# An attention and state-space kernel: other TensorE work is placed into planned waits as soon as it can go, and its allowance counts each round's products

## The chip, the core and the metric

The kernel runs on one core of a Trainium2 chip. The metric is device time in microseconds (us) from the launch to the end of the program. Three runs of the kernel before took 1277.9, 1279.32 and 1282.04 us; the median is 1279.32 us. The engines are called PE (TensorE), DVE (VectorE), ACT (ScalarE), POOL (GpSimd) and SP (SyncE, which issues most transfers). Each takes its instructions strictly in the order in which the program lists them.

## What is computed

Two unrelated results are joined side by side: `outa`, a long convolution whose filter comes from a state-space model, and `outb`, attention with 32 heads that share one set of keys and values.

```python
# a: D = 576 channels, L = 2048 positions, N = 128 states
K = einsum("dn,dnl,dn->dl", Cc, exp(dt * A * l), dB).real   # complex powers: exp, sin, cos
y = irfft(rfft(u, 2L) * rfft(K, 2L))[:L] + u * Dskip
# b: S = 2048 positions, 32 heads of 18, one k and one v for all heads
q = x @ wq;  k = x @ wk;  v = x @ wv
o = softmax(q k^T * 18**-0.5) v
out = concat([y, o.reshape(S, 576) @ wo], -1)
```

## The kernel before

**The attention in rounds.** The attention is cut into 1024 tiles: 4 chunks of 512 queries, 16 pairs of heads in each, and 16 blocks of 128 keys. For each tile PE computes two 128x512 scores into a PSUM tile `s` (`scores`, L384, two matmuls), ACT takes their exponentials into `P` (`exponentials`, L392), and for every two tiles PE multiplies `P` by the values into `ops` (`product`, L664, four matmuls). There are three `s` buffers (NS) and six `P` buffers (NP). The loop in `main` therefore goes by rounds of three tiles: three scores, one or two products (a product takes two tiles, so the rounds alternate), and the exponentials. The scores of a round wait for the exponentials of the round before to free their `s` buffers.

**Other work.** Everything else has to find a place beside this. On PE these are pieces of 0.1 to 0.75 us by the program's own costs: the query projections (`q`, L157), the output projections (`op`, L157), the filter tables of the convolution (`kg`, L976), and the transforms of its signal and filter (`hu`, `lu`, `hk`, `lk`, `iy`, L157). They share one PSUM bank, `ps_f`: a piece that begins a new result has to wait until DVE has read the one before out of it. DVE carries most of the convolution as long rows of elementwise instructions. The convolution goes by 12 blocks of 48 channels. For each block ACT has to leave the exponentials once and compute a cosine and a sine (`r` at L905, `f` at L906), with a table load ahead of them and another one behind (L905, L392).

**The order of the work.** PE, DVE and ACT run an order that the program writes out itself while it is built. Generators yield after every piece, and `Stream` wraps one of them: `side` (query projections and output projections), `prep` (scaling of finished heads), and two for the convolution (`front` for the filter of the next block, `back` for the current one). What a generator yields is a kind, a time from which the next piece is ready, and whether it holds the bank. Kind "p" is a piece for PE, "v" for DVE, "w" waits for a later round, and "b" is the cosine and sine, which `Conv.go` lets go as soon as at least 8 pieces of projections are in hand (`beside`), or after 16 key blocks. A `Clock` estimates the time of PE, DVE and ACT (`K.t`, `K.v`, `K.a`); `K.fill` is when the shared bank is free, by this estimate. DVE's estimate is 0.085 us for an instruction and 1.04 ns for each element of a row (`Clock.dve`, `Vector`).

**Where other work is put.** `fill(then)` is called ahead of every product and ahead of each round's scores; `then` is when that next step can go. It offers the streams their turn until none can go. Pieces for PE need credit: an allowance that each round raises (the rest of TOTAL spread over the rest of the loop, within bounds) and each piece lowers, or time that is left before `then`. A stream whose next piece is not ready at `K.t` is passed over, and is not looked at again until the next call, which may be behind the next scores. RATE and PACE say how much DVE work of the convolution may be, and should be, done by each step.

**The end.** When the loop is over, the last products are issued, then whatever is left of the output projections, and then `finish`, which scales the last heads (`rc_last`, L521 and L511 on DVE) and adds the last parts of `outb`.

## Time and profile before

| what | value |
|---|---|
| median of three runs | 1279.32 us |
| the profiled execution | 1282.59 us, span from first to last instruction 1280.8 us |
| PE busy | 1174.6 us, 92% of the span |
| ACT busy | 1045.9 us, 82% |
| DVE busy | 991.2 us, 77% |
| POOL busy | 226.6 us, 18% |
| mean granted TensorE clock | 0.972 of full speed |

A row of the timeline gives the start, the time that the instructions take together, the engine, the line, what is written and read, and in square brackets how long the engine had been idle and what ended that. Two program matmuls of this kind count as four in it (x4): the trace counts each float32 matmul twice, except those of the scores. Starts are more reliable than ends on PE, since matmuls overlap and their ends are modelled. A row of the windows gives for each engine the busy time and the count in a stretch, then the granted clock and the transfers.

The first scores start 33.6 us after the span's start, the last ones at 1261.3 us.

### The profile page before, as it was taken

The page shows a single profiled execution, that of the slowest core. Times are in us where ns is not written, and L with a number is a line of the kernel's source. Part 1 is how long each engine was busy: PE and PEld are TensorE (multiplying, and loading weights), DVE is VectorE, ACT ScalarE, POOL GpSimd, SP SyncE. Part 2 cuts the span into 40 slices and gives each one's busy share as a digit, 9 for nine tenths or more (in the row PEclk, how much of TensorE's full clock was granted, in tenths as well). Part 3 has the DMA queues.
Part 4 walks back from the last instruction along what each step waited for, and adds up shares of the span by engine and source line. Part 5 has one row for each costly group of instructions (what it writes and reads, how often), then busy time and mean ns, then how long its engine had stood idle before and what let it go on. Part 6 is the DMA issues. An engine that isn't in the chain of part 4 may idle for free.

```text
span 1280.8 us, 32948 instructions
## 1 busy us (share of the span) xinstructions
PE 1174.6 (92%) x13762; PEld 481.4 (38%) x13762; DVE 991.2 (77%) x1612; ACT 1045.9 (82%) x1101; POOL 226.6 (18%) x450
## 2 busy tenths in 40 slices
PE   5799799899999899999899899899899999899997
PEld 1234234334334344344334344334344334333433
DVE  4565985896797887897798887897795797798673
ACT  2488987898998888988788888788887978987884
POOL 3262002214110030230051030041050120020000
PEclk9799899899999899999899899899999999999999
DMA  7522013012021011212023012022012212012111
GB/s 216 173 50 60 14 37 104 22 57 73 24 67 58 19 48 64 64 39 98 18 73 99 10 38 74 10 77 80 17 38 96 78 36 68 21 26 74 51 39 40
DMA packets 56922, 75.35 MB, mean 59 GB/s; under 512 B 19536, under 2 KB 30160, under 8 KB 56256
## 3 DMA queue, kind: packets, MB, share of 16 engines
q1 hardware_dynamic: 35784, 58.22, 13.8%
q0 software_dynamic: 20288, 14.39, 5.1%
q8 instruction: 110, 1.80, 0.6%
q10 hardware_dynamic: 696, 0.58, 0.1%
q14 instruction: 44, 0.36, 0.1%
HBM read 35.28 MB, written 22.54 MB: 45 GB/s over the span
## 4 chain that ended last, share of the span: by engine, by line
PE 64%; ACT 15%; issue 10%; DVE 5%; DMA 3%; SPq 1%; POOL 1%; ACTq 0%; DVEq 0%; POOLq 0%
PE ops L664 27%; PE s L384 19%; ACT P L392 12%; PE op L157 5%; PE q L157 5%; PE iy L157 2%; PE kg L976 2%; DVE tab L95 2%; DMA xr<-xT 2%; SPq L265 1%; ACT L392 1%; ACT f L906 1%; PE hu L157 1%; PE lu L157 1%; PE hk L157 1%
## 5 line engine op out<-in xcount | busy, mean ns | idle before, releaser
L392 ACT ACTIVATE P<-s 128x1024 f32<-128x1024 f32 x1024 | 967.2, 1032 | 200.5 <-PE s L384 175.1
L664 PE MATMUL ops<-P,v_sb 128*32 128x512 f32 x4096 | 544.4, 606 | 3.7 <-DVE o L99 2.9
L384 PE MATMUL s<-aug,kaug 55*128 55x512 f32 x2048 | 378.6, 450 | 79.0 <-ACT P L392 75.3
L384 PEld LDWEIGHTS s<-aug,kaug 55*128 55x128 f32 x2048 | 174.4, 187 | 379.6 <-ACT P L392 335.1
L348 POOL DMA_DIRECT2D aug<-qh x252 | 126.4, 510 | 677.6 <-DVE qh L99 428.1
L664 PEld LDWEIGHTS ops<-P,v_sb 128*32 128x32 f32 x4096 | 109.8, 110 | 130.3 <-issue 92.0
L157 PE MATMUL q<-x,wq_sb 128*32 128x256 f32 (+2 forms) x1480 | 112.2, 417 | 0.0
L157 PE MATMUL op<-wo_sb,oT 126*32 126x288 f32 (+1 forms) x1152 | 88.7, 421 | 1.0 <-DVE part L99 0.3
L374 POOL DMA_DIRECT2D aug<-sh x61 | 33.0, 548 | 231.4 <-DVE sh L103 231.3
L157 PEld LDWEIGHTS q<-x,wq_sb 128*32 128x32 f32 (+1 forms) x1480 | 48.8, 115 | 65.2 <-issue 41.6
L348 POOL DMA_DIRECT2D aug<-ql x128 | 65.0, 514 | 5.1 <-issue 5.1
L99 DVE COPY ksb<-kg 128x192 f32<-128x192 f32 x48 | 17.5, 364 | 56.1 <-PE kg L976 56.1
L95 DVE TENSOR_TENSOR tab<-tab,tt 128x576 f32<-128x576 f32 (+1 forms) x72 | 59.1, 821 | 1.7
L95 DVE TENSOR_TENSOR tab<-tab 128x576 f32<-128x576 f32 (+1 forms) x72 | 59.0, 819 | 1.1
L95 DVE TENSOR_TENSOR tab<-sum,r 128x576 f32<-128x576 f32 (+1 forms) x72 | 58.8, 816 | 0.0
L95 DVE TENSOR_TENSOR tt<-f,sum 128x576 f32<-128x576 f32 (+1 forms) x72 | 58.7, 815 | 0.0
L95 DVE TENSOR_TENSOR tab<-r,dif 128x576 f32<-128x576 f32 (+1 forms) x72 | 58.6, 814 | 0.0
L157 PEld LDWEIGHTS op<-wo_sb,oT 126*32 126x32 f32 (+1 forms) x1152 | 34.1, 112 | 59.9 <-issue 28.4
L95 DVE TENSOR_TENSOR sck<-lk,sck 128x384 f32<-128x384 f32 x48 | 24.5, 552 | 31.7 <-PE lk L157 31.7
L95 DVE TENSOR_TENSOR acc<-acc,pt 128x1728 f32<-128x1728 f32 (+2 forms) x36 | 48.6, 1350 | 0.2
L95 DVE TENSOR_TENSOR pt<-us,ks 128x1728 f32<-128x1728 f32 (+2 forms) x36 | 48.6, 1350 | 0.1
L976 PEld LDWEIGHTS kg<-tab 128*32 128x32 f32 x2304 | 37.8, 110 | 27.4 <-issue 13.0
(118 smaller groups left out, 1001.9 us busy)
## 6 DMA issues: line engine op xcount, KB each, us to landing
aug<-qh POOLq DMA_DIRECT2D x252, 36.0 KB, 1.9
od<-o SPq DMA_DIRECT2D x31, 256.0 KB
aug<-ql POOLq DMA_DIRECT2D x128, 36.0 KB, 2.1
u<-u SPq DMA_DIRECT2D x12, 384.0 KB
kd<-ksb SPq DMA_DIRECT2D x12, 384.0 KB
kt<-kd SPq DMA_DIRECT2D x48, 96.0 KB
outa<-u SPq DMA_DIRECT2D x12, 384.0 KB
oT<-od SPq DMA_DIRECT2D x16, 252.0 KB
```

The source lines that it names most:

```text
L95: return self.v.tensor_tensor(out, *a, **k)
L99: return self.v.tensor_copy(out, *a, **k)
L157: nc.tensor.matmul(ps[j:e], w[:, j:e], x, start=start, stop=stop, tile_position=(0, j))
L265: nc.sync.dma_start(self.kaug[b + r:b + r + 18, c * CT:(c + 1) * CT].bitcast(F32), t[32 * c:32 * c + 18, :].bitcast(F32))
L348: q.dma_start(t[b:b + 18, :], src[r:r + 18, :])
L374: nc.gpsimd.dma_start(self.aug[(c, h // 2)][54:119:64, :], sh)
L384: nc.tensor.matmul(ps[:, j, :], self.kaug[r, kb * P:(kb + 1) * P], t[r, :], start=True, stop=True)
L392: nc.scalar.activation(pt, ps, AF.Exp, scale=SCALE)
L664: nc.tensor.matmul(o_ps[32 * j:32 * j + 32, :], self.v[:, kb, :], pts[2 * n + j // 2][:, j % 2, :], start=(kb == 0), stop=(kb == 15), tile ...
L906: nc.scalar.activation(f, f, AF.Sin, scale=TWO_PI)
L976: nc.tensor.matmul(ps[32 * g:32 * g + 32, d, :], t[:, :32], t[:, 32:], start=(j == 0), stop=(j == 1), tile_position=(0, 32 * g))
```

## The change

`fill` no longer gives up when no stream can go at `K.t`. It asks each stream with the new `Stream.event` when it will be able to go. If the earliest such time lies over 0.5 us ahead of `then`, it sets `K.t` to that time and offers the turns again. The time skipped (`idle`) is not charged against the credit. So a piece can now be listed ahead of the next scores although it has to wait for DVE or for the bank first.

The allowance counts products: each product lowers the credit by 0.96, and each round raises it by 1.5 times 0.96 on top of the share for other work, so that a round with two products leaves less for other work than a round with one. The bounds of the share, of the credit, and the four constants RATE, PACE, TOTAL and the floor of the credit change as well.

```diff
-RATE = 1.75
-PACE = 1.68
+RATE = 1.9
+PACE = 1.8
 AHEAD = 0.8
-TOTAL = 340.0
+TOTAL = 330.0
...
+    def event(self):
+
+        if not self.live or self.kind in "wb":
+            return 0.0
+        if self.kind == "v":
+            return max(self.ready, self.k.v - self.ahead) + 1e-6
+        return self.ready if self.holds else max(self.ready, self.k.fill)
...
         def fill(then):
 
-            t = K.t
+            t, idle = K.t, 0.0
             more = True
             while more:
                 more = False
-                credit = state["credit"] - (K.t - t)
+                credit = state["credit"] - (K.t - t - idle)
...
                         more = True
                         break
+                else:
+
+                    at = min((x for x in (st.event() for st in [prep, side] + conv.streams) if x > K.t), default=then)
+                    if at < then - 0.5:
+                        idle += at - K.t
+                        K.t = at
+                        more = True
+            t += idle
             if K.t > t:
 
                 K.t += 0.1
             state["filled"] += K.t - t
-            state["credit"] = max(state["credit"] - (K.t - t), -0.4)
+            state["credit"] = max(state["credit"] - (K.t - t), -0.8)
...
             K.pe(0.96, done[2 * n + 1] + 0.1, self.o_free if kb == 0 else 0.0)
+            state["credit"] -= 0.96
...
-            state["credit"] = min(state["credit"] + NS / 2 * min(max((TOTAL - state["filled"]) / max(LAST - s, 20), 0.45), 0.7 if s < 384 else 0.9), 1.5)
+
+            state["credit"] = min(state["credit"] + NS / 2 * (0.96 + min(max((TOTAL - state["filled"]) / max(LAST - s, 20), 0.45), 0.62 if s < 384 else 0.68)), 0.5 + 0.96)
```

The same instructions are issued, in another order. The two pieces below show what that does on PE at two places.

The first place is PE around the ninth cosine and sine. ACT has them behind the exponential `P_13_10` before and behind `P_12_12` now. Three more score tiles find a free buffer then; the fourth needs one that only an exponential behind the cosine and sine frees. That fourth tile is `s_13_12` before and `s_12_14` now. `s_13_12` is the score tile of the head pair 13 and the key block 12, `ops_6` the product for the heads of group 6, `lk` a transform of the filter, `op_2_1` a piece of the output projection, and `up` a small part of a query's bound. Before:

```order
L384 MATMUL s_12_11_10239<-aug_119,kaug 128x512 x2
L384 MATMUL s_13_11_10242<-aug_111,kaug 128x512 x2
L384 MATMUL s_12_12_10245<-aug_119,kaug 128x512 x2
L664 MATMUL ops_6_10034<-P_12_9_10175,v_sb 32x512 x2
L664 MATMUL ops_6_10034<-P_13_9_10217,v_sb 32x512 x2
L157 MATMUL lk_10258<-kt_9998,dft_sb 32x192 x8
L664 MATMUL ops_6_10034<-P_12_10_10219,v_sb 32x512 x2
L664 MATMUL ops_6_10034<-P_13_10_10221,v_sb 32x512 x2
L384 MATMUL s_13_12_10275<-aug_111,kaug 128x512 x2
L384 MATMUL s_12_13_10278<-aug_119,kaug 128x512 x2
L384 MATMUL s_13_13_10281<-aug_111,kaug 128x512 x2
L157 MATMUL op_2_1_10305<-wo_sb,oT_7345 32x288 x12
```

And now:

```order
L392 MATMUL s_13_12_10273<-aug_111,kaug 128x512 x2
L392 MATMUL s_12_13_10276<-aug_119,kaug 128x512 x2
L392 MATMUL s_13_13_10279<-aug_111,kaug 128x512 x2
L165 MATMUL op_2_1_10293<-wo_sb,oT_7353 32x288 x20
L680 MATMUL ops_6_10034<-P_12_11_10236,v_sb 32x512 x2
L680 MATMUL ops_6_10034<-P_13_11_10238,v_sb 32x512 x2
L165 MATMUL up_0_10348<-sel_sb,aw_0_10340 32x8 x4
L392 MATMUL s_12_14_10362<-aug_119,kaug 128x512 x2
```

Before, `op_2_1` begins behind the scores that wait; now all 20 of its matmuls (five groups of four) stand ahead of the scores that wait, beside one product.

The second place is the end of the loop on PE. `s_15_15` is the last score tile, `ops_7` the last product, `op_1_1_2` to `op_3_1_2` pieces of the output projection of the last chunk, and `fin` the first matmuls of `finish`. Before:

```order
L664 MATMUL ops_7_14030<-P_14_11_14242,v_sb 32x512 x2
L664 MATMUL ops_7_14030<-P_15_11_14244,v_sb 32x512 x2
L157 MATMUL op_3_1_2_14293<-wo_sb,oT_13117 32x288 x4
L384 MATMUL s_14_14_14299<-aug_119,kaug 128x512 x2
L384 MATMUL s_15_14_14302<-aug_111,kaug 128x512 x2
L384 MATMUL s_14_15_14305<-aug_119,kaug 128x512 x2
```

And now, from the last products on:

```order
L680 MATMUL ops_7_14012<-P_14_15_14274,v_sb 32x512 x2
L680 MATMUL ops_7_14012<-P_15_15_14289,v_sb 32x512 x2
L165 MATMUL op_1_1_2_14305<-wo_sb,oT_13239 32x288 x4
L165 MATMUL op_2_0_2_14311<-wo_sb,oT_13239 32x288 x4
L165 MATMUL op_2_1_2_14317<-wo_sb,oT_13239 32x288 x4
L165 MATMUL op_3_0_2_14323<-wo_sb,oT_13239 32x288 x4
L165 MATMUL op_3_1_2_14329<-wo_sb,oT_13239 32x288 x4
L165 MATMUL fin_14339<-wo_sb,oT_13239 32x288 x8
```

Before, the last piece of the output projection stood ahead of the scores `s_14_14`; now five pieces stand behind the last product, each with its addition on DVE, and the additions stand ahead of `rc_last` on DVE.

Each of the 11 blocks whose cosine and sine fall into the loop has such a place. Counted in the same way, the other work that stands on PE ahead of the first scores that wait for ACT's return, and behind the scores that can still go, was this before and now. A `q` or an `op` is a group of three or four matmuls that run side by side, an `lk`, `hk` or `lu` two such groups. (In block 4 the work stands one tile earlier, and is counted there.)

| block | before | now |
|---|---|---|
| 1 | none | half an `lk`, 10 `q` |
| 2 | one `lk` | 7 `q` |
| 3 | 10 `q` | 7 `q` |
| 4 | one `lk` | one `hk`, one `lk`, 5 `op` |
| 5 | 10 `q` | half an `lu`, 10 `q` |
| 6 | one `lk` | 7 `q` |
| 7 | one `up` | two `lk`, one `hk`, 5 `q` |
| 8 | one `lk` | two `lk`, one `hk`, 3 `q` |
| 9 | one `lk` | 5 `op`, one `up` |
| 10 | 7 `q` | 7 `q` |
| 11 | one `lk` | 5 `op`, one `up` |

The rounds of the loop that hold no other work at all are 48 of 341 before and 51 now.

## The prediction

> **What bounds the kernel now.** I read the page's costliest groups first, then the windows over the loop, then the timeline around each cosine and sine on ACT. In the groups stand the two steps that hand rounds to each other, the exponentials and the scores:

> ```profile
> L392 ACT ACTIVATE P<-s 128x1024 f32<-128x1024 f32 x1024 | 967.2, 1032 | 200.5 <-PE s L384 175.1
> L384 PE MATMUL s<-aug,kaug 55*128 55x512 f32 x2048 | 378.6, 450 | 79.0 <-ACT P L392 75.3
> ```

> Both wait for each other: ACT 175.1 us for scores, PE 75.3 us for exponentials. Over the whole loop PE is the busier one:

> ```profile
> 57.00:1262.00 1205.00, 1127.46 (x13366) 463.27 (x13368) 956.50 (x1544) 1026.58 (x1081) 214.30 (x424) 0.98 0.17 52
> ```

> PE is idle for 1205 - 1127.46 = 77.5 us, ACT for 178, DVE for 249. The amount of work on PE does not change, so what an order can win is these 77.5 us and what a lower clock costs. Where they lie is seen in 20 us around each of the 11 cosines and sines; the columns behind the length are busy PE, weight loads, DVE, ACT, POOL, then the granted clock:

> ```profile
> 146.00:166.00 20.00, 14.73 (x102) 4.60 (x94) 19.62 (x34) 18.17 (x19) 5.12 (x10) 0.83 0.09 25
> 225.00:245.00 20.00, 15.35 (x146) 6.08 (x148) 15.82 (x24) 16.97 (x18) 0.00 (x0) 0.83 0.04 14
> 327.00:347.00 20.00, 18.82 (x196) 7.31 (x188) 18.62 (x25) 19.55 (x20) 3.93 (x8) 1.00 0.05 12
> 421.00:441.00 20.00, 14.60 (x142) 5.78 (x136) 16.73 (x23) 15.28 (x16) 0.00 (x0) 0.83 0.04 16
> 519.00:539.00 20.00, 18.45 (x194) 7.44 (x190) 18.59 (x30) 19.27 (x20) 7.17 (x14) 1.00 0.29 89
> 615.00:635.00 20.00, 15.08 (x132) 5.92 (x136) 17.44 (x27) 15.41 (x16) 0.00 (x0) 0.83 0.05 14
> 712.00:732.00 20.00, 15.39 (x148) 6.12 (x148) 18.70 (x31) 16.09 (x16) 1.62 (x3) 0.83 0.01 2
> 810.00:830.00 20.00, 15.09 (x121) 5.90 (x124) 17.38 (x27) 15.67 (x16) 0.00 (x0) 0.83 0.00 1
> 905.00:925.00 20.00, 15.33 (x138) 5.72 (x138) 17.06 (x27) 16.64 (x18) 1.31 (x3) 0.91 0.04 16
> 1017.00:1037.00 20.00, 18.57 (x200) 7.15 (x192) 19.65 (x30) 16.72 (x17) 3.49 (x7) 0.91 0.07 17
> 1109.00:1129.00 20.00, 15.89 (x147) 6.71 (x142) 15.89 (x24) 16.60 (x18) 0.00 (x0) 0.91 0.04 15
> ```

> Two kinds show. In blocks 3 and 5 PE is busy for over 18 us and keeps the full clock. In eight others it is busy for 14.6 to 15.9 us, and the clock falls. ACT's part in the first of them is this, two table loads and two activations:

> ```profile
> 147.76 1.28 ACT L905 ACT_TABLE_LOAD   x1
> 149.05 1.33 ACT L905 ACTIVATE r<-r,hp_sb 128x1248 f32<-128x1248 f32 x1
> 150.29 1.23 ACT L906 ACTIVATE f<-f 128x1248 f32<-128x1248 f32 x1
> 151.54 1.28 ACT L392 ACT_TABLE_LOAD   x1
> ```

> No exponential ends for 5.1 us. PE at the same place:

> ```profile
> 145.48 1.92 PE L664 MATMUL ops<-P,v_sb 128*32 128x512 f32 x16
> 147.33 0.96 PE L384 MATMUL s<-aug,kaug 55*128 55x512 f32 x6
> 148.22 1.06 PE L664 MATMUL ops<-P,v_sb 128*32 128x512 f32 x8
> 153.91 2.63 PE L384 MATMUL s<-aug,kaug 55*128 55x512 f32 x6 [4.62 <-ACT P L392]
> 156.47 3.14 PE L664 MATMUL ops<-P,v_sb 128*32 128x512 f32 x16
> ```

> PE has one product to do, then stands for 4.62 us. Behind that the same three score tiles take 2.63 us instead of 0.96, the same two products 3.14 instead of 1.92: 1.67 + 1.22 = 2.9 us more at half clock. So an uncovered cosine and sine costs the wait and then the clock. The other blocks in pieces:

> ```profile
> 329.62 4.52 PE L157 MATMUL q<-x,wq_sb 128*32 128x256 f32 x80
> ...
> 429.06 0.79 PE L384 MATMUL s<-aug,kaug 55*128 55x512 f32 x2 [5.40 <-ACT P L392]
> ...
> 811.52 0.83 PE L157 MATMUL lk<-kt,dft_sb 128*32 128x192 f32 x16
> ...
> 1018.99 3.23 PE L157 MATMUL q<-x,wq_sb 128*32 128x256 f32 x56
> ...
> 1023.67 0.50 PE L384 MATMUL s<-aug,kaug 55*128 55x512 f32 x2 [0.59 <-ACT P L392]
> ...
> 1025.50 0.50 PE L384 MATMUL s<-aug,kaug 55*128 55x512 f32 x2 [0.41 <-ACT P L392]
> 1025.93 3.60 PE L664 MATMUL ops<-P,v_sb 128*32 128x512 f32 x16
> ...
> 1031.33 1.67 PE L157 MATMUL op<-wo_sb,oT 126*32 126x288 f32 x24
> ...
> 1116.26 0.50 PE L384 MATMUL s<-aug,kaug 55*128 55x512 f32 x2 [3.04 <-ACT P L392]
> ```

> Eight blocks wait like the first, from 3.04 us (block 11) to 5.40 us (block 4); the eight sum to 33.3 us, 4.2 us in the mean. Block 3 has ten `q` in that place and no wait at all; block 10 has seven and waits 0.59 us, and still its clock falls, though for less: two products take 3.60 us instead of 1.92, 1.7 us more. With that 0.6 the 11 blocks wait for 33.9 of the 77.5 us. The clock falls for long in six (0.83) and shortly in three (0.91): 6 x 2.9 + 3 x 1.7 = 22.5 us.

> **The change part by part.** *Waits at the 11 blocks.* Sizes first: ten `q` take 4.52 us, 0.43 each; an `op` takes (1.67 - 0.67) / 2 = 0.5 us, from the row of three above and that of one at 1253.58 below; an `lk` or `hk` 0.83 us with some 0.17 us of drain at its end, so 0.66. The order puts in front of the waiting scores: block 1 ten `q`, 4.3 us; blocks 2, 3, 6 and 10 seven `q`, 3.0 each; block 4 five `op` and an `hk`, of which I count the `op`, 2.5; block 5 ten `q`, 4.3; block 7 three transforms and five `q`, 4.2; block 8 three transforms and three `q`, 3.3; blocks 9 and 11 five `op`, 2.5 each. Taken from a wait of 4.2 us (5.4 in the fourth I leave at 4.2, since its `hk` counts too): 0 + 4 x 1.2 + 1.7 + 0 + 0 + 0.9 + 2 x 1.7 = 10.8 us are left. Saved: 33.9 - 10.8 = 23.1 us. Bounds: 15 us if ACT's absence is felt for a microsecond longer in most blocks; 33.9 at most.

> This is time only if the pieces leave rounds in which PE was the later one. They do: the order holds 48 rounds without other work before and 51 now, so the rounds in which PE waits for ACT anyway are as many as they were, and the pieces come out of the loaded ones. Three more empty rounds, at a wait like the 0.41 above, cost 1.2 us.

> *The clock.* Every wait over 4.2 us was followed by a long fall, those of 3.04 and 3.12 us by a short one, the 0.59 with two of 0.41 behind it by a short one, full cover by none. With at most 1.7 us left I expect no long fall, and a short one in six of the eight blocks that still wait: 6 x 1.7 = 10.2. Saved: 22.5 - 10.2 = 12.3 us. Bounds: 7 us (all eight, and one long) and 22.5 (none).

> [...]

> *The end of the loop.* Five `op` now stand behind the last product, each with an addition on DVE, one bank between them:

> ```profile
> 1253.58 0.67 PE L157 MATMUL op<-wo_sb,oT 126*32 126x288 f32 x8
> ...
> 1254.93 0.67 PE L157 MATMUL op<-wo_sb,oT 126*32 126x288 f32 x8
> ...
> 1263.50 1.87 PE L157 MATMUL fin<-wo_sb,oT 126*32 126x288 f32 x24
> ```

> ```profile
> 1254.32 0.46 DVE L95 TENSOR_TENSOR part<-part,op 128x288 f32<-128x288 f32 x1 [2.10 <-PE op L157]
> ...
> 1264.10 0.42 DVE L521 TENSOR_SCALAR rc_last<-ops 128x256 f32<-128x256 f32 x1 [5.06 <-PE ops L664]
> ```

> An `op`, its addition and the next `op` are 1254.93 - 1253.58 = 1.35 us apart. The first would start where `fin` starts now, 1263.50; the fifth addition ends 4 x 1.35 + 0.74 + 0.46 = 6.6 us later, at 1270.1. `rc_last` stands behind it on DVE, and the rest of the end behind `rc_last`: 1270.1 - 1264.1 = 6.0 us later. The five leave the loop, 5 x 0.5 = 2.5 us of PE. Net 3.5 us lost; between 2.5 (the loop gains their latency too) and 6 (the loop gains nothing).

> *Waits that the planner now plans.* A piece that is listed ahead of scores although the bank is not free yet lets PE stand at it, with the scores and products queued behind, and ACT behind those. It costs nothing while the estimate for DVE holds. It runs short:

> ```profile
> L95 DVE TENSOR_TENSOR acc<-us,ks 128x2304 f32<-128x2304 f32 x12 | 30.6, 2551 | 0.1
> L95 DVE TENSOR_TENSOR sv<-acc 128x384 f32<-128x384 f32 x48 | 24.3, 548 | 0.1
> ```

> ```profile
> 337.14 0.68 DVE L99 CAST qh<-q 126x512 fp32r<-126x512 f32 x1
> ```

> The program reckons 0.085 + 2304 x 0.00104 = 2.48 us and 0.48 us for these, 0.07 us less than each takes. Behind five or six such instructions a piece comes 0.4 us late. The trace of before does not show how often that will hold scores up; nothing if the piece ends before the scores could go, 0.4 us if not. Ten times 0.4, 4 us, is my estimate; bounds 0 and 12 us (thirty times). It can't be below nothing, since the piece is no earlier for being waited for.

> *The rest.* The even allowance takes work from rounds with two products and gives it to those with one; with six `P` buffers between them PE has done this averaging already wherever no wait shows, so I give it nothing, bounded by 5 us of gain. RATE and PACE let DVE's work run ahead; DVE is idle for 249 us in the loop, so it hides there. Moved transfers on SP are loads and stores with a block's length ahead of their use, and POOL's order is as before.

> *Sum.* -23.1 + 1.2 - 12.3 + 3.5 + 4 = -26.7 us. The profiled execution took 1282.6 us, so 1255.9 us; it lies 3.3 us above the median, which gives 1252.6 us for a median.

> **The rivals.** *The clock comes back whole.* If a short fall needs a wait of about 3 us, as in blocks 9 and 11, and block 10 was an accident, no block falls. Then 10.2 us more are won: 1242.4 us. For it: four of the blocks will wait no more than block 10 did. Against: block 10.

> *The waits only move.* If the pieces pulled into the 11 blocks are missed in rounds that have just enough now, the 23.1 us come back as many waits like that 0.41 us; it would take 56 of them. The clock still gains. Time: 1252.6 + 23.1 = 1275.7 us. Against it: the count of empty rounds, 48 and 51.

> *Slower: DVE late where PE now waits for it.* The cast of block 3's `q` ran at 337.14 us, although the ten `q` from 329.62 on had ended by 334.1: DVE was in long rows of the convolution, 3 us. A piece listed behind such a wait, with scores behind it, holds PE and then ACT for these 3 us, where before it was simply listed later. The gain without the 4 us is 30.7; ten such stalls eat it up, sixteen make 48 us and 1279.3 - 30.7 + 48 = 1297 us. Against it: the program knows of these rows and counts them, so only what it misjudges is late.

> **How the numbers follow.** Forecast 0.60, the whole clock 0.19, the moved waits 0.14, DVE late 0.07. What a measurement of this kernel can tell from no change is about 0.3%, 3.8 us, so "same" is 1275.5 to 1283.2 us. Of the moved waits about half lie inside that; of late DVE one part in seven does: same 0.08, slower 0.06, faster 0.86. The forecast's own range, with its bounds taken two at a time, is 1240 to 1266 us. The range that leaves 2 in 10 out reaches from 1238 us, below the whole clock, to 1271 us, short of the moved waits.

> **What would show it.** In the profile after, at each of the 11 places a row of `q`, `op` or transforms between the last free scores and the waiting ones, with under 2 us of wait behind it; windows of 20 us there with PE busy for 17 us or more and a clock of 0.91 or 1.00; PE's idle time in the loop near 55 us; `rc_last` 6 us behind the last product; waits of PE for DVE longer than now, but of tenths of a microsecond. I am wrong if clocks of 0.83 stay, if PE's waits for `P` outside the blocks grow by 20 us, or if waits of PE for DVE of 2 us and more stand ahead of scores.

## The result and the profile after

The changed kernel takes 1250.01 us (median of 6 runs, 1249.24 to 1253.37) against 1279.70 us of six runs before: a ratio of 0.977, with a 95% interval of 0.9754 to 0.9785. Its profiled execution took 1249.9 us, with a span of 1248.1 us against 1280.8. The forecast was 1252.6 us.

The loop first, from 57 us to the start of the last scores (1261.3 us before, 1223.2 us now); the columns are those of the same view before:

```profile
57.00:1223.00 1166.00, 1106.85 (x13316) 458.49 (x13312) 952.70 (x1536) 1026.10 (x1080) 215.19 (x424) 0.99 0.18 54
```

To that last start before, 57 to 1261, PE was busy for 1126.46 of 1204 us and idle for 77.5. Now it is busy for 1106.85 of 1166 and idle for 59.2. So of the 38 us by which the loop got shorter, 18.4 are idle time and 19.6 are busy time. Of the busy time, 2.5 us are five `op` that left the loop; most of the rest is the clock, as shown below. Then the 20 us around each of the 11 cosines and sines on ACT:

```profile
120.00:140.00 20.00, 18.33 (x192) 7.50 (x184) 17.31 (x26) 19.39 (x20) 7.42 (x15) 1.00 0.21 55
223.00:243.00 20.00, 17.55 (x170) 6.25 (x158) 19.72 (x25) 19.75 (x21) 8.95 (x18) 1.00 0.19 47
314.00:334.00 20.00, 18.27 (x182) 6.75 (x174) 19.62 (x22) 19.55 (x21) 5.52 (x11) 1.00 0.05 11
407.00:427.00 20.00, 17.85 (x220) 7.58 (x212) 17.95 (x26) 18.47 (x19) 0.00 (x0) 1.00 0.04 17
490.00:510.00 20.00, 18.76 (x214) 8.41 (x216) 16.98 (x30) 19.17 (x20) 5.99 (x12) 1.00 0.27 89
599.00:619.00 20.00, 18.24 (x218) 7.44 (x212) 19.55 (x24) 18.22 (x19) 8.41 (x17) 1.00 0.14 33
686.00:706.00 20.00, 16.86 (x208) 7.71 (x206) 15.74 (x25) 17.86 (x18) 0.00 (x0) 1.00 0.01 2
779.00:799.00 20.00, 16.86 (x164) 7.09 (x160) 14.66 (x24) 15.21 (x16) 0.08 (x1) 0.83 0.04 15
877.00:897.00 20.00, 17.42 (x192) 7.32 (x188) 18.68 (x29) 17.47 (x18) 1.62 (x3) 0.91 0.05 17
987.00:1007.00 20.00, 18.79 (x216) 7.74 (x212) 19.72 (x26) 18.36 (x19) 4.82 (x10) 1.00 0.07 15
1072.00:1092.00 20.00, 17.43 (x180) 7.32 (x172) 18.32 (x29) 17.55 (x18) 2.15 (x4) 0.91 0.04 15
963.00:983.00 20.00, 17.35 (x170) 6.74 (x168) 12.94 (x24) 15.90 (x18) 4.49 (x9) 0.91 0.27 86
```

The first 11 rows are the blocks. PE is busy for 196.4 of their 220 us, where it was 177.3: idle time in the blocks fell from 42.7 to 23.6 us, by 19.1. Outside them it went from 77.5 - 42.7 = 34.8 to 59.2 - 23.6, some 35.5 us. So all of the idle time that was won was won in the blocks, and hardly any of it came back elsewhere. The clock stood at 0.83 in six blocks and at 0.91 in three; now 0.83 is seen once (block 8) and 0.91 twice (blocks 9 and 11). The twelfth row is a new fall that belongs to no block.

What the falls cost can be read more closely. In windows cut to the stretches with a granted clock of 0.50, nine in the loop before (six of 6.83 us, three of 3.41) and four now (one and three), the sums are, before and after:

```profile
sum 51.21, PE 45.25 PEld 16.88 DVE 49.93 ACT 36.13 POOL 1.17; mean PE 5.03 PEld 1.88 DVE 5.55 ACT 4.01 POOL 0.13
sum 17.06, PE 15.68 PEld 6.01 DVE 13.26 ACT 10.42 POOL 3.51; mean PE 3.92 PEld 1.50 DVE 3.32 ACT 2.60 POOL 0.88
```

PE was busy for 45.25 us at half clock, of which full clock would have saved half, 22.6 us; now it is 7.8 us. Both are estimates from the busy time and the granted clock of 0.50; two products took 3.60 us in such a stretch of before (1025.93) and 1.92 us at full clock (145.48). So 14.8 us of the busy time are the clock. With the 2.5 us of `op` that leaves 2.3 us of the 19.6 for which the traces show no cause; the ends of matmuls, and so the busy time, are modelled.

What PE waits for, the largest rows after:

```profile
PE s L392 <- ACT P L400: 36.5, 98, 5.9
...
PE ops L680 <- DVE o L99: 6.2, 9, 2.1
PE up L165 <- DVE aw L103: 4.3, 4, 1.7
PE q L165 <- DVE sck L95: 3.7, 3, 1.2
```

The columns are the time in total, how often, and the longest. The wait for exponentials fell from 75.3 us by 38.8, twice what the idle time did: part of it has become waits for DVE. The waits in the loop by engine, counted where they end, from the traces (p1, p4, p7 and p9 are runs of the next section):

| run | blocks, for ACT | blocks, for DVE | between, for ACT | between, for DVE |
|---|---|---|---|---|
| before | 41.9 | 0 | 27.2 | 5.6 |
| after | 7.7 | 15.6 | 22.9 | 12.0 |
| p1 | 7.7 | 22.3 | 25.5 | 17.4 |
| p4 | 10.0 | 17.1 | 29.3 | 20.3 |
| p7 | 9.1 | 13.9 | 27.8 | 9.7 |
| p9 | 27.7 | 4.2 | 29.6 | 4.5 |

Block 8 on PE shows how a wait for ACT becomes waits for DVE:

```profile
780.62 0.86 PE L165 MATMUL lk<-kt,dft_sb 128*32 128x192 f32 x16
782.72 0.86 PE L165 MATMUL hk<-kt,dft_sb 128*32 128x192 f32 x16 [1.24 <-DVE sck L95]
784.24 1.50 PE L165 MATMUL lk<-kt,dft_sb 128*32 128x192 f32 x16 [0.67 <-DVE sck L99]
786.98 3.20 PE L165 MATMUL q<-x,wq_sb 128*32 128x256 f32 x21 [1.24 <-DVE sck L95]
```

Ahead of the scores that waited for ACT now stand three transforms and the `q`, and all but the first wait for DVE to clear the one bank: 1.24 + 0.67 + 1.24 = 3.15 us. The wait for ACT has gone, but 3.15 us of idle time lie in the same place, and the clock falls among them: the second `lk` takes 1.50 us, the first took 0.86.

The end of the loop on PE:

```profile
1224.17 1.90 PE L680 MATMUL ops<-P,v_sb 128*32 128x512 f32 x16
1225.88 0.67 PE L165 MATMUL op<-wo_sb,oT 126*32 126x288 f32 x8
...
1230.94 0.69 PE L165 MATMUL op<-wo_sb,oT 126*32 126x288 f32 x8 [0.57 <-DVE part L95]
```

And on DVE:

```profile
1231.70 0.46 DVE L95 TENSOR_TENSOR part<-part,op 128x288 f32<-128x288 f32 x1 [0.81 <-PE op L165]
...
1232.13 0.40 DVE L529 TENSOR_SCALAR rc_last<-ops 128x256 f32<-128x256 f32 x1
```

The last products before stood here on PE:

```profile
1261.76 2.30 PE L664 MATMUL ops<-P,v_sb 128*32 128x512 f32 x16
```

The five `op` are (1230.94 - 1225.88) / 4 = 1.27 us apart. `rc_last` starts 7.96 us behind the start of the last products; before it was 1264.10 - 1261.76 = 2.34 us, and the 5.6 us more are the pieces' turns. From the last scores to the end of the span it is 24.9 us, where it was 19.5.

In spans: -19.1 in the blocks, +0.7 between them, -14.8 of clock, -2.3 of busy time without a known cause, and 5.4 - 2.5 = +2.9 for the end: -32.6, where the span fell by 32.7.

### The profile page after: what moved, and what is told of

The parts are those of the page before. It is cut to its first block, busy times and chain, and to the rows that moved or that the text cites. A ratio compares the mean times of both kernels' runs of the same rounds, so it can differ in the third digit from the quotient of the medians.

```text
span 1248.1 us, 32953 instructions
## 1 busy us (share of the span) xinstructions
PE 1158.3 (93%) x13762; PEld 477.2 (38%) x13762; DVE 991.0 (79%) x1612; ACT 1045.6 (84%) x1101; POOL 227.5 (18%) x450
## 4 chain that ended last, share of the span: by engine, by line
PE 65%; DVE 14%; ACT 12%; issue 5%; DMA 3%; SPq 1%; ACTq 0%; DVEq 0%
PE ops L680 27%; PE s L392 19%; ACT P L400 10%; PE q L165 5%; PE op L165 4%; PE kg L994 3%; PE iy L165 2%; DVE tab L95 2%; DVE ks L95 2%; DVE acc L95 2%; DMA xr<-xT 2%; PE hu L165 1%; PE hk L165 1%; PE lk L165 1%; DVE pt L95 1%
## 5 line engine op out<-in xcount | busy, mean ns | idle before, releaser
L392 PE MATMUL s<-aug,kaug 55*128 55x512 f32 x2048 | 367.6, 443 | 39.6 <-ACT P L400 36.5
L392 PEld LDWEIGHTS s<-aug,kaug 55*128 55x128 f32 x2048 | 171.1, 185 | 353.2 <-ACT P L400 318.3
L165 PE MATMUL q<-x,wq_sb 128*32 128x256 f32 (+2 forms) x1480 | 108.5, 407 | 5.2 <-DVE sck L95 3.7
L165 PE MATMUL op<-wo_sb,oT 126*32 126x288 f32 (+1 forms) x1152 | 84.8, 409 | 6.7 <-DVE part L95 2.3
L95 DVE TENSOR_TENSOR tab<-tab,tt 128x576 f32<-128x576 f32 (+1 forms) x72 | 59.1, 821 | 1.6
L95 DVE TENSOR_TENSOR tab<-tab 128x576 f32<-128x576 f32 (+1 forms) x72 | 58.9, 818 | 1.0
L95 DVE TENSOR_TENSOR tab<-sum,r 128x576 f32<-128x576 f32 (+1 forms) x72 | 58.7, 816 | 0.0
L95 DVE TENSOR_TENSOR tt<-f,sum 128x576 f32<-128x576 f32 (+1 forms) x72 | 58.7, 815 | 0.0
L95 DVE TENSOR_TENSOR tab<-r,dif 128x576 f32<-128x576 f32 (+1 forms) x72 | 58.7, 815 | 0.0
L99 DVE COPY ksb<-kg 128x192 f32<-128x192 f32 x48 | 17.4, 362 | 50.9 <-PE kg L994 50.4
L95 DVE TENSOR_TENSOR acc<-acc,pt 128x1728 f32<-128x1728 f32 (+2 forms) x36 | 48.5, 1348 | 0.2
L95 DVE TENSOR_TENSOR pt<-us,ks 128x1728 f32<-128x1728 f32 (+2 forms) x36 | 48.6, 1349 | 0.0
L95 DVE TENSOR_TENSOR sck<-lk,sck 128x384 f32<-128x384 f32 x48 | 24.5, 552 | 27.9 <-PE lk L165 27.9
```

The lines of the kernel that those rows point to most:

```text
L95: return self.v.tensor_tensor(out, *a, **k)
L99: return self.v.tensor_copy(out, *a, **k)
L165: nc.tensor.matmul(ps[j:e], w[:, j:e], x, start=start, stop=stop, tile_position=(0, j))
L392: nc.tensor.matmul(ps[:, j, :], self.kaug[r, kb * P:(kb + 1) * P], t[r, :], start=True, stop=True)
```

## The experiments

Theory A was that the look ahead (`event`) carries the gain: it lets pieces be listed into ACT's absence, and the clock follows. The rivals lay the gain on the counted allowance, or on RATE and PACE. One table for all runs, from the same views: "loop" is from 57 us to the last scores, "blocks" PE's idle time in the 20 us around the 11 departures of ACT, "between" its idle time in the rest of the loop, "end" from the last scores to the span's end. The blocks' windows are whole microseconds and lie a little differently against each departure, which is worth some 0.3 us in these two columns. The ratio is to the kernel before, which had medians of 1280.9 to 1281.1 us beside them.

| run | loop | PE busy | blocks | between | end | median | ratio, 95% interval |
|---|---|---|---|---|---|---|---|
| before | 1204 | 1126.5 | 42.7 | 34.8 | 19.5 | 1279.7 | 1 |
| after | 1166 | 1106.9 | 23.6 | 35.5 | 24.9 | 1250.0 | 0.977, 0.9754 to 0.9785 |
| p1 look ahead | 1191 | 1115.0 | 31.6 | 44.5 | 18.9 | 1267.3 | 0.9894, 0.9873 to 0.9914 |
| p2 counting | 1167 | 1103.2 | 27.3 | 36.5 | 89.5 | 1315.8 | 1.0277, 1.0255 to 1.03 |
| p3 RATE, PACE | 1219 | 1131.8 | 47.6 | 39.7 | 19.3 | 1297.9 | 1.0136, 1.0112 to 1.016 |
| p4 look ahead, RATE, PACE | 1198 | 1120.0 | 27.4 | 50.6 | 19.3 | 1274.6 | 0.9946, 0.9929 to 0.9964 |
| p5 after, end folded | 1168 | 1108.7 | 23.3 | 36.0 | 21.7 | 1247.2 | 0.9743, 0.9724 to 0.9763 |
| p6 p5, no cover | 1195 | 1115.6 | 48.0 | 31.4 | 42.9 | 1298.6 | 1.0141, 1.0125 to 1.0156 |
| p7 p5, old bounds | 1169 | 1107.4 | 23.4 | 38.2 | 21.0 | 1249.5 | 0.9757, 0.9742 to 0.9772 |
| p8 before, clock held | 1192 | 1137.6 | 18.9 | 35.5 | 19.3 | 1269.8 | 0.9914, 0.9899 to 0.9929 |
| p9 p5, ample count, no look ahead | 1180 | 1111.2 | 33.2 | 35.7 | 24.8 | 1263.5 | 0.9862, 0.9847 to 0.9878 |
| p10 p5, RATE and PACE of before | 1155 | 1096.5 | 20.2 | 38.3 | 32.4 | 1247.3 | 0.974, 0.9725 to 0.9755 |
| p11 p5, later `begin` | 1168 | 1108.5 | 23.3 | 36.3 | 21.7 | 1248.4 | 0.9752, 0.9738 to 0.9765 |

### The parts alone

**p1, the look ahead alone.** After, with the allowance and the constants of before:

```diff
-RATE = 1.9
-PACE = 1.8
-TOTAL = 330.0
+RATE = 1.75
+PACE = 1.68
+TOTAL = 340.0
...
-            state["credit"] = max(state["credit"] - (K.t - t), -0.8)
+            state["credit"] = max(state["credit"] - (K.t - t), -0.4)
...
-            state["credit"] -= 0.96
...
-            state["credit"] = min(state["credit"] + NS / 2 * (0.96 + min(..., 0.62 if s < 384 else 0.68)), 0.5 + 0.96)
+            state["credit"] = min(state["credit"] + NS / 2 * min(..., 0.7 if s < 384 else 0.9), 1.5)
```

> Only the look ahead in `fill` is taken over; the credit, its bounds and RATE, PACE and TOTAL are those of before. Theory A (the gain lies in the 11 places where ACT is away for the cosine and sine, in the waits there and in the clock that falls behind them): the order fills nine of the 11 with 2.6 to 4.7 us of work and the other two with about 2, nothing is left behind the last product, so 1245 to 1252 us, as good as the whole change or some us better. Rival B (the gain comes from the even load of the rounds, which the credit that counts products brings): 1265 to 1280 us.

1267.3 us: well above what theory A gave, and inside the rival's 1265 to 1280. The blocks are covered in part, as theory A says, 42.7 to 31.6 us. What it left out is between them: 44.5 us idle instead of 34.8. The order has 77 rounds without other work, 48 before and 51 after. Two rows of its waits (the only wait of an `lk` or `hk` before was one of 0.9 us):

```profile
PE hk L165 <- DVE sck L95: 7.2, 8, 1.2
PE lk L165 <- DVE sck L99: 6.8, 10, 0.7
```

Pieces are now listed where they must wait for DVE. By the table of the waits, all that PE waits longer between the blocks than before is for DVE (17.4 us instead of 5.6); its waits for ACT there are no longer (25.5 and 27.2).

**p2, the counted allowance alone.** After, without the look ahead, RATE and PACE of before:

```diff
-RATE = 1.9
-PACE = 1.8
+RATE = 1.75
+PACE = 1.68
...
-                    if at < then - 0.5:
+                    if False:
```

> Only the credit that counts products, with its bounds and TOTAL; no look ahead, RATE and PACE of before. The order covers seven of the 11 places more or less, but leaves 21 pieces of the output projection and the end of the last convolution block behind the last product. Theory A: the places save some 16 us of waits and 8 us of clock, the long end costs about 18 us net, so 1268 to 1280 us. Rival B (even rounds are the gain): the loop itself is shorter by more than 40 us and the total is below 1262 us in spite of the end.

1315.8 us, not the 1268 to 1280 expected. The loop is as short as that of after, 1167 us. But it did not do all the work: 21 `op` and the last part of the convolution stand in the end, which takes 89.5 us.

```profile
1229.27 0.69 PE L165 MATMUL op<-wo_sb,oT 126*32 126x288 f32 x8 [2.48 <-DVE sck L95]
...
1264.01 1.19 PE L165 MATMUL op<-wo_sb,oT 126*32 126x288 f32 x8 [0.58 <-DVE part L95]
...
1291.48 2.79 PE L165 MATMUL iy<-w,dft_sb 128*32 128x192 f32 x32 [22.00 <-DVE w L95]
```

The pieces go one by one, each behind its addition, at half clock (1.19 us each instead of 0.69), and then `iy` waits for 22.00 us for a chain of DVE's long rows that nothing covers any more. So part of the short loop is work put off. Another part is real: PE's idle time in the loop fell from 77.5 to 63.8 us, since the order happens to cover more of the blocks (27.3 us idle instead of 42.7). What it puts off costs far more in the end.

**p3, RATE and PACE alone.** Look ahead off, allowance of before; only the two constants are new.

```diff
...
-                    if at < then - 0.5:
+                    if False:
...
-            state["credit"] -= 0.96
...
```

> Only RATE 1.9 and PACE 1.8. The order leaves the 11 places as they were before, all but one or two. Theory A: 1275 to 1284 us, no difference. Rival C (DVE's work of the convolution running ahead is what puts work in hand where ACT is away): 1260 us or less.

1297.9 us, 17 us slower than before, where 1275 to 1284 was expected, and far from the rival's 1260. Block 5, which ten `q` covered before, is bare (4.3 us idle instead of 1.6), and so is block 10; the clock stands at 0.83 in nine blocks. Earlier DVE work does not help by itself; here it changes which blocks happen to be covered.

**p4, look ahead with RATE and PACE.** After, with the allowance of before:

```diff
...
-            state["credit"] -= 0.96
...
```

> The look ahead and RATE and PACE, with the credit and TOTAL of before. The order fills all 11 places but the first with 2.6 to 4.3 us, and nothing is left behind the last product. Theory A: 1243 to 1251 us; the 5 or 6 us that the end of the whole change costs are not paid, so this should be some us below 1250. Rival B: 1262 us or more, since the credit does not count products.

1274.6 us; theory A's 1243 to 1251 failed again, and in the same way, and the rival's 1262 or more came true. The blocks are covered nearly as in after (27.4 us), but between them PE is idle for 50.6 us, with 81 rounds without other work. So theory A holds for the blocks alone. For the look ahead without the count, the rival "the waits only move" is right in size: in p4, 15.3 us less in the blocks, 15.8 more between.

Why they come back is not shown. One reading is that the look ahead takes work from rounds that are then empty: over the runs the idle time between the blocks goes with the number of empty rounds (41 in p6, 64 in p7, 77 in p1, 81 in p4, with 31.4, 38.2, 44.5 and 50.6 us). But what PE waits for there in p4 is mostly DVE, 20.3 us instead of 5.6 before, and little more for ACT, 29.3 instead of 27.2. No run here separates the two readings, nor tells how the counted allowance brings the waits for DVE down to 12.0 us in after.

### With the end out of the way

**p5, the end folded in.** The five late `op` are accumulated with `fin`, in its bank, so that no addition on DVE stands ahead of `rc_last`:

```diff
+                if self.closing and ms[0] > 0:
+                    self.merged[t, n] = self.merged.get((t, n), []) + list(ms)
+                    continue
...
-            matmul4(nc, ps[t, nh], o[:126, 3, ...], self.wo[:126, 3, cols[nh]], start=True, stop=False)
+            ms = self.merged.get((t, nh), []) + [3]
+            for m in ms:
+                matmul4(nc, ps[t, nh], o[:126, m, ...], self.wo[:126, m, cols[nh]], start=(m == ms[0]), stop=False)
```

> The whole change, but the five pieces of the output projection that are left behind the last product are not issued by themselves: their matmuls go into the PSUM tiles of `fin`, ahead of those for the last heads, so that they need no addition and no bank of their own. If the end costs what I worked out (6 us later at `rc_last`, measured 5.6), the time falls by 4.5 to 6 us against the whole change: 1243.5 to 1246 us. Rival (the end is set by the transfers and the additions behind it, the pieces lie beside them): 1249 to 1251 us.

1247.2 us, 2.9 less than after, where 4.5 to 6 was expected; the intervals of the two ratios overlap. In the trace the end is 3.2 us shorter (21.7 instead of 24.9). PE at the end:

```profile
1225.89 1.90 PE L686 MATMUL ops<-P,v_sb 128*32 128x512 f32 x16
1227.61 4.55 PE L165 MATMUL fin<-wo_sb,oT 126*32 126x288 f32 x72
1232.09 0.70 PE L526 MATMUL bc<-rc_last,b 128*128 128x256 f32 x2
```

And DVE there:

```profile
1227.86 0.42 DVE L535 TENSOR_SCALAR rc_last<-ops 128x256 f32<-128x256 f32 x1 [1.21 <-PE ops L686]
1228.32 1.75 DVE L525 RECIPROCAL rc_last<-rc_last 128x256 f32<-128x256 f32 x1
```

`rc_last` follows the last products at once and its reciprocal ends at 1230.1, but `bc`, which reads it, starts at 1232.09: it stands behind 4.55 us of `fin`. The additions no longer delay `rc_last`; some 2 of the 5.6 us that this gains are taken by the next wait, which is PE's own order. The next five runs start from p5, so that work put off does not blur them.

**p11, one pair of `begin` later.** P5, with the third pair of `fin` moved behind the first outputs:

```diff
-        for t in range(3):
+        def pair(t):
...
+        for t in range(2):
+            pair(t)
...
+        pair(2)
```

> The folded run with the last two of its first six groups of `fin` moved behind the second `bc`. In the folded run the matmul `bc` starts 2 us after its data are there, behind 4.55 us of `fin`. 1245 to 1246.5 us, 0.7 to 2 us below the folded run's 1247.15, if that is what kept the fold from its full 5 us; 1247 or more if another step of the end is the late one.

`bc` starts at 1230.03, 2.06 us earlier, and yet the time does not fall to the 1245 to 1246.5 expected (1248.4 us; the intervals of both overlap). The postponed `fin` now stands ahead of the last outputs at 1234.93, for 3.10 us. The end holds that much work on PE; this other order of it gains nothing.

**p6, no cover.** P5, with the look ahead only where at most 2 us are to be filled, so that it doesn't act in the blocks:

```diff
-                    if at < then - 0.5:
+                    if at < then - 0.5 and then - t <= 2.0:
```

> As the run with the folded end, but `fill` looks ahead only where the scores can go within 2 us, so never in the 11 places where ACT is away. The order fills two of the 11 with 2 us or more and leaves the others as before; the rounds without other work are fewer (41). Theory A: the waits of the 11 places are back near 37 us in 12 us each, the clock falls there in eight or nine, so 25 to 32 us above the folded run, 1268 to 1276 us. Rival B (even rounds are the gain): at most 12 us above it, below 1257 us.

The loop is 27 us longer than in p5, the blocks idle for 48.0 us instead of 23.3, and the clock stands at 0.83 in eight of them. In time it is 51 us (48.6 in the profiled spans), where 25 to 32 was expected, for the end grew by 21 (42.9 us instead of 21.7) with work that the loop no longer took. The cover of the blocks is worth at least these 27 us of loop, since p6's loop also holds less work; the rest is the price of work put off, as in p2.

**p7, the old bounds.** P5, with the bounds of the share and TOTAL as before, the product still counted:

```diff
-TOTAL = 330.0
+TOTAL = 340.0
...
-... 0.62 if s < 384 else 0.68)
+... 0.7 if s < 384 else 0.9)
```

> As the run with the folded end, but with the bounds of the share (0.7 and 0.9) and TOTAL of before; the products are still counted. The order covers all 11 places; the rounds without other work are 64 instead of 51, and 58 instead of 43 rounds hold over 3.6 us of PE work. If the empty rounds decide what the look ahead is worth, 3 to 10 us above the folded run, 1247 to 1255 us; if only the count of the products matters, within 2 us of it.

1249.5 us, 2.3 above p5, with intervals that overlap: between "within 2 us" and "3 to 10 us", so no cost of the old bounds is shown. The counting keeps most of the gain without the new bounds.

**p9, ample work without look ahead.** P5 without look ahead, with so large a share that nothing is put off:

```diff
-TOTAL = 330.0
+TOTAL = 360.0
...
-                    if at < then - 0.5:
+                    if False:
...
-... 0.62 if s < 384 else 0.68)
+... 0.8 if s < 384 else 1.0)
```

> With the folded end. The products are counted, but there is no look ahead; the bounds of the share are wider (0.8 and 1.0, TOTAL 360), so that the allowance does not leave work behind as in the run with the credit alone. The order covers places 2 to 8 of the 11 and not 1, 9, 10 and 11. If both parts are needed (the look ahead for the places where ACT is away, the count for the rounds between them): four uncovered places at 3.4 us of wait and 2.9 us of clock more, 25 us, less what places 7 and 8 gain: 1262 to 1272 us. If the count alone carries the gain: 1246 to 1254 us.

1263.5 us, inside the 1262 to 1272 expected. Between the blocks PE idles for 35.7 us, as in p5, but four blocks (1, 9, 10 and 11) have no cover, idle for 4.3 to 4.7 us and show 0.83. Block 1:

```profile
127.32 2.62 PE L393 MATMUL s<-aug,kaug 55*128 55x512 f32 x6 [4.04 <-ACT P L401]
129.88 1.93 PE L686 MATMUL ops<-P,v_sb 128*32 128x512 f32 x8
```

This is the first block of before again. So without look ahead the rest (the counted allowance with work enough, RATE and PACE, the folded end) brings 1281 down to 1263.5, and the look ahead the other 16 us, 12 of them in the loop, where four blocks stay bare without it.

**p10, RATE and PACE of before.** P5, with RATE 1.75 and PACE 1.68:

```diff
-RATE = 1.9
-PACE = 1.8
+RATE = 1.75
+PACE = 1.68
```

> With the folded end; the whole change but RATE and PACE of before. All 11 places are covered, the rounds are as even as with the change (39 with over 3.6 us). What is left behind the last product is eight pieces, folded, and the last transform of the convolution with its additions. If RATE and PACE only serve to get the convolution done in time: the loop is as short as with the folded run (1168 us from 57 us on, within 4), and the end is 5 to 12 us longer: 1250 to 1260 us. If running ahead is a gain of its own: loop over 8 us longer.

1247.3 us, the same as p5, where 1250 to 1260 was expected. The loop, expected within 4 us of p5's, is 13 us shorter, and the end 10.7 us longer: the constants shift work between the two.

### The clock by itself

**p8, the clock held.** The kernel before, with eight groups of matmuls added after ACT's departure where the round had under 2 us of other work. They read what lies there and nothing reads their result; they only keep PE busy:

```diff
...
+            if self.away == r // NS and holder() is None and state["filled"] - f0 < 2.0:
+                idle = self.ps_f.tile([P, CT], F32, tag="f", name=f"idle{r}")
+                for _ in range(8):
+                    matmul4(nc, idle[:, 0:256], self.wq[0][:, 0, :], conv.dft[:, 0:256])
...
```

> The kernel before, its order unchanged, with 32 useless matmuls (3.4 us) added in each of the eight places where PE waits 3 us or more for ACT; their results are not used. The waits are still lost, but PE is not idle in them. If the fall of the clock is a cost of its own (22.5 us by the rows of before), most of that comes back: 1259 to 1267 us. If the slow stretches behind the waits lie beside ACT's work and cost nothing, 1277 to 1284 us.

1269.8 us against 1280.9 of before beside it: 11 us won, where 14 to 22 was expected, by work that does nothing. PE in block 6:

```profile
615.79 3.66 PE L157 MATMUL idle<-dft_sb,wq_sb 128*32 128x256 f32 x64 [0.38 <-DVE sck L95]
619.65 0.50 PE L385 MATMUL s<-aug,kaug 55*128 55x512 f32 x2 [0.20 <-ACT P L393]
```

And the loop:

```profile
57.00:1249.00 1192.00, 1137.61 (x13870) 474.68 (x13866) 955.85 (x1544) 1025.36 (x1080) 214.14 (x424) 1.00 0.18 52
```

The added matmuls take 8 x 3.65 = 29.2 us; without them PE is busy for 1108.4 us, 18.1 less than before, for the same work. Idle time and added work together are 54.4 + 29.2 = 83.6 us, 6.1 more than the 77.5 of before: the additions wait for DVE's bank and hold scores back a little. 18.1 - 6.1 = 12.0, which is the loop's 1204 - 1192. So the falls of the clock are a cost of their own, beside the waits ahead of them, and in this order 18 us of it went with the waits filled. (Two short falls are left here: the 0.91 in blocks 1 and 2.)

## Why the prediction was right, and where it was off

**What bounds the kernel.** Right. PE was the busier engine, and what an order could win was its idle time and its clock. Both show in the result, 18.4 and 14.8 us, and nothing else of that size does.

**The waits at the blocks, and those the planner plans.** Their sum was right, each of them was not. The text took 23.1 us from the blocks, gave 4 back for waits at DVE, and 1.2 for three more empty rounds: -17.9. Measured, -19.1 in the blocks and +0.7 between: -18.4. But PE's waits for exponentials fell by 38.8 us, and its waits for DVE in the loop rose from 5.6 to 27.6 us (the table of the waits), by 22.0, beyond the upper bound of 12 us. The step that was off is the size of that term. It reckoned with ten late pieces of 0.4 us, for errors in the estimate for DVE. What the trace shows instead is waits of 0.67 and 1.24 us at the bank between one transform and the next, as in block 8, which the planner knows and accepts. They cost little because 15.6 of the 22.0 us lie in the blocks, where PE would have waited for ACT: the pieces stand there in place of the wait. The other 6.4 us, between the blocks, stand against 4.3 us less for ACT. That the two errors cancel is luck in part: the cover had been counted as pure work, without the waits inside it. One reading there was loose: ACT runs no exponential for 5.1 us in block 1, and with 1.03 us for the next one their ends lie 6.1 us apart; the sum went by PE's waits and does not change.

**The clock.** That shorter waits bring fewer falls was right, nine in the loop before and four now, and the size a little too small: 12.3 us, measured 14.8, inside its bounds of 7 and 22.5. The prices were right: the half-clock rows give 22.6 us for the falls of before, where the text had 22.5, with 2.9 us for a long fall in the mean and 1.7 for a short one. The windows of 20 us would give (1 - 0.83) x 20 = 3.4 us for a long one, but that counts half clock in which PE stood still: in block 1 it was busy for 4.96 of the 6.83 us. What was off is the falls that are left. Six short ones were expected, 10.2 us; it is one long and three short, of which one short one lies outside the blocks, 7.8 us. That a long fall stayed had not been expected. The 2.3 us of busy time beside it stay open, and so does a like difference in p1: its falls (0.83 in one block, 0.91 in three) cost 7.9 us by the same estimate, so its PE should be busy for 14.7 us less than before, and is for 11.5.

The rival with the whole clock back, 1242.4 us, took it that a short fall needs a wait of about 3 us, as in blocks 9 and 11 of before (3.12 and 3.04 us). The trace after refutes it: no wait of that length stands ahead of the fall in block 9, which the row of the last product shows (1.93 us where 1.06 is usual):

```profile
879.49 2.63 PE L165 MATMUL op<-wo_sb,oT 126*32 126x288 f32 x40 [0.34 <-DVE sck L95]
...
884.67 0.25 PE L165 MATMUL up<-sel_sb,aw 126*32 126x8 f32 x8 [1.68 <-DVE aw L103]
884.85 1.13 PE L392 MATMUL s<-aug,kaug 55*128 55x512 f32 x4
886.40 0.61 PE L392 MATMUL s<-aug,kaug 55*128 55x512 f32 x2 [0.42 <-ACT P L400]
886.94 1.93 PE L680 MATMUL ops<-P,v_sb 128*32 128x512 f32 x8
```

Waits of 1.68 and 0.42 us close ahead, and one of 0.34 us some 7 us before, are all that PE shows there. When the falls begin, as far as the traces show it, is told in the last section.

**The end of the loop.** Right: `rc_last` 6.0 us later expected, 5.6 measured; net 3.5 expected, 2.9 measured. The pieces are 1.27 us apart, not 1.35. P5 adds what the text did not see: without them, PE's own `fin` is the next thing late, and the end in the trace is 3.2 us shorter, not 5.6.

**The rest.** The text gave RATE and PACE nothing, and p10 bears it out. It gave the even allowance nothing either, since "PE has done this averaging already". The number held, the reason did not: between the blocks PE is idle for as long as before (34.8 and 35.5 us), but with the look ahead and without the allowance for longer (p1 44.5, p4 50.6). The allowance is a condition of the look ahead, which the text did not see. The count of empty rounds, 48 and 51, had already that effect in it; the text used it as evidence without asking which part of the change kept it so.

**The rivals.** "The waits only move" is refuted for the whole change and true in size for p4, the look ahead without the count, though there they come back mostly as waits for DVE. DVE late by 2 us and more ahead of scores happened once, in products behind `o` at 971.88:

```profile
971.88 1.89 PE L680 MATMUL ops<-P,v_sb 128*32 128x512 f32 x8 [2.15 <-DVE o L99]
```

One clock of 0.83 stayed. Both had been named as signs of a wrong prediction, and both appear singly.

P5 and p10 are the fastest, at 1247.2 and 1247.3 us; their intervals overlap with that of after (1250.0), so they are not shown to be better than it.

## What to carry to other kernels

When one engine leaves a tight hand-over for a few microseconds, list other work of its partner ahead of the first instruction that will wait, even if that work must itself wait a little: a wait in its place cost little new here (15.6 of the 22.0 us of new waits for DVE lie in the blocks), though the clock still fell among such waits (0.83 in block 8, 0.91 in block 9). Then look at the rounds beside it: without the counted allowance the look ahead only moved the waits (15.3 us off the blocks, 15.8 on between them in p4). And judge an order by its whole span: p2 and p10 have a loop that is as short as that of after, or shorter, and left work for an end where nothing covers it; p2 was slower than before by it, and p10 gained nothing over p5.

## What the runs showed of the hardware

The wait ahead alone did not decide here whether the clock fell. After and p5 have the same order in the loop. In block 2 of after PE waits three times, and the clock stays up:

```profile
230.68 0.49 PE L392 MATMUL s<-aug,kaug 55*128 55x512 f32 x2 [0.57 <-ACT P L400]
231.60 0.50 PE L392 MATMUL s<-aug,kaug 55*128 55x512 f32 x2 [0.42 <-ACT P L400]
232.51 0.49 PE L392 MATMUL s<-aug,kaug 55*128 55x512 f32 x2 [0.41 <-ACT P L400]
232.94 1.06 PE L680 MATMUL ops<-P,v_sb 128*32 128x512 f32 x8
```

In p5 the same waits are followed by a fall, as the product shows:

```profile
228.77 0.51 PE L393 MATMUL s<-aug,kaug 55*128 55x512 f32 x2 [0.55 <-ACT P L401]
229.69 0.49 PE L393 MATMUL s<-aug,kaug 55*128 55x512 f32 x2 [0.41 <-ACT P L401]
230.61 0.50 PE L393 MATMUL s<-aug,kaug 55*128 55x512 f32 x2 [0.42 <-ACT P L401]
231.04 1.74 PE L686 MATMUL ops<-P,v_sb 128*32 128x512 f32 x8
```

```profile
227.88:231.29 3.41, 2.03 (x14) 0.72 (x14) 3.34 (x5) 3.41 (x4) 0.87 (x2) 1.00 0.02 5
231.29:234.70 3.41, 3.41 (x18) 0.99 (x14) 3.38 (x5) 3.11 (x5) 3.41 (x8) 0.50 0.33 73
```

In after the same waits come 1.9 us later and spread over the same two stretches (163 and 162 times 3.413 us ahead of its fall at 784.25), with PE busy for 2.73 and 2.69 us. But idle time alone does not tell the two apart: around block 8, from 779 to 799 us, PE is idle for 3.66 us in p5 and for 3.14 us in after, and it is in p5 that the clock stays up. So waits of this size had a fall behind them in one run and none in the other, and what decides stays open. Over the six runs of after the time goes with the clock, from 1249.24 us at 0.986 to 1253.37 us at 0.981. And in the end of p2 an `op` took 0.69 us at 1229.27 and 1.19 us each from 1232.21 to 1264.01 us, with PE busy for 1.19 of every 1.77 us; the granted clock is 0.64 in the mean from 1222 to 1313 us. In these 32 us the pieces with a wait after each did not bring it back.
